# A fused attention and two-layer mixture kernel: ranks by counting matmuls, a short token chunk in two products, a tile's pieces in another order

## The chip, the core and the metric

The kernel runs on one core of one Trainium2 chip. The metric is the device time of one execution in microseconds; lower is better. TensorE (PE) multiplies, VectorE (DVE), ScalarE (ACT) and GpSimd (POOL) work element by element, SyncE (SP) starts most transfers. Each engine takes its instructions strictly in program order and waits at each for the semaphores of what it needs.

## What is computed

Three layers follow one another: thresholded attention, a mixture of eight experts with a sticky routing, and a mixture of four causal attention experts. The second is the one that the change touches:

```python
for b in range(4):                       # x: 4 x 576 tokens of 512
    prev_e = -1
    for s in range(576):
        fresh_e = int(np.argmax(logits[b, s]))
        if s == 0 or local_gate[b, s] < 0.5:
            e = fresh_e
        else:
            e = prev_e if prev_e >= 0 else fresh_e
        prev_e = e
        h = np.maximum(x[b, s] @ w1[e], 0.0)     # 512 -> 1024
        out[b, s] = p[e] * (h @ w2[e])           # 1024 -> 512
```

So a token either takes the expert of its own largest logit or keeps the one of the token before it, and only the chosen expert's two layers are computed for it.

## The kernel before

**Stage 1** runs attention on 16 pairs of heads. An order written out by hand gives every step of a pair a due time in units of one score tile, nine to a pair; due times sort the instructions of all engines. For one pair the scores go to one of three score banks (line 246), VectorE takes the row's extreme (257) and, when ScalarE has the exponentials (267), forms the kept values (280), which frees the bank. TensorE transposes them (293) into a pool of two banks that everything else of stage 1 shares, ScalarE evicts them (304), and TensorE multiplies by the values (336). A product with the identity and the gate weights (368) turns the result into token rows and logits; ScalarE evicts it (386), and GpSimd scales it by the reciprocal sums (393), which line 357 on GpSimd and line 360 on VectorE prepare. The last pair does that scaling of the logits on VectorE (384).

**The early routing** (`Route.early`) handles the first three batches while stage 1 still computes the fourth. It is a list of steps, each with a due time in `EARLY`; a step that yields a second part (an eviction) has two. A pair of 24-row tables (three batches by eight experts, 576 tokens long) is scanned into a one-hot table O of each token's expert (line 609). The running count of O along the tokens is a second scan, in two halves (617). Three small matmuls (624 to 626) give the totals; `most` (639 to 650) finds the most frequent expert, whose number `e0` starts the loads of the first tile's weights (`W0`, line 952), and six values `n0` that limit the tiles. `value` and `place` (655 to 672) pick each token's rank by five matmuls; `split_rank` splits it into a row and a column of a tile; `column` and `hot` (680 to 698) make one-hot tables on GpSimd; `invert` (704, 705) multiplies them into token numbers, by which GpSimd gathers the first tile's rows.

**The last routing** (`Route.main`) adds the fourth batch. The chain on VectorE is long, and TensorE fills it with pieces of the first expert tile: 16 pieces of the first layer, 16 of the second, each a handful of products. `FILL` says how many go between two steps. The remaining ones are dealt out by `LEFT`: before each of the three transposes (`tx`, line 984) of the second tile's gathered chunks, pieces run until so many are left. The second of these transposes takes a bank of a PSUM pool that opens where the router's own pool closes; the last read of the router's pool is line 873 on VectorE.

**The expert tiles** hold 256 tokens, or 288 (the first of the second kind) and 352. Every product is done in three passes of a split number: high by high, high by low, low by high. `g1` computes the first layer, `hT_ev` evicts it as high and low halves (ScalarE 1006, VectorE 1007), `y_mm` (1040) computes the second layer with a chunk of at most 128 tokens as the stationary side and 512 columns streamed, `y_ev` evicts and stores it.

## Time and profile before

| | us |
|---|---|
| three runs | 756.20, 756.21, 756.98 |
| median | 756.21 |
| the profiled execution, its own time | 758.47 |
| its span | 756.7 |
| TensorE busy in the span | 727.2 (96%) |
| VectorE, ScalarE, GpSimd busy | 545.3, 490.3, 285.6 |

The span is what the trace covers of one execution; the rest of its time lies around it. A busy TensorE is a modelled figure: products overlap, so the distance from one start to the next is the cost of one, not its duration. In the timelines a row gives start, busy time, engine, line, operation, what it writes and reads, shapes and count, and in square brackets the idle time ahead of it with what released it.

### The profile page before, as it was taken

The page shows a single profiled execution, that of the slowest core. Times are in us where ns is not written, and L with a number is a line of the kernel's source. Part 1 is how long each engine was busy: PE and PEld are TensorE (multiplying, and loading weights), DVE is VectorE, ACT ScalarE, POOL GpSimd, SP SyncE. Part 2 cuts the span into 40 slices and gives each one's busy share as a digit, 9 for nine tenths or more (in the row PEclk, how much of TensorE's full clock was granted, in tenths as well). Part 3 has the DMA queues.
Part 4 walks back from the last instruction along what each step waited for, and adds up shares of the span by engine and source line. Part 5 has one row for each costly group of instructions (what it writes and reads, how often), then busy time and mean ns, then how long its engine had stood idle before and what let it go on. Part 6 is the DMA issues. An engine that isn't in the chain of part 4 may idle for free.

```text
span 756.7 us, 14216 instructions
## 1 busy us (share of the span) xinstructions
PE 727.2 (96%) x5061; PEld 614.3 (81%) x5061; DVE 545.3 (72%) x1424; ACT 490.3 (65%) x1024; POOL 285.6 (38%) x435
## 2 busy tenths in 40 slices
PE   5999999999999898899999999999999999999996
PEld 4787888888887677697899899889888888888874
DVE  6998998999988987713745555654268888887781
ACT  5888887888887685223555455544256877777783
POOL 6888888888776880300101000100156000000000
PEclk9999999999999999999999999999999999999998
DMA  8439443443432620295457647701233000100103
GB/s 278 145 116 316 139 141 122 159 131 114 130 114 65 239 62 17 84 367 176 160 201 248 219 168 261 261 0 53 61 105 102 10 16 1 43 15 29 43 29 102
DMA packets 37408, 95.40 MB, mean 126 GB/s; under 512 B 4336, under 2 KB 14832, under 8 KB 33232
## 3 DMA queue, kind: packets, MB, share of 16 engines
q1 hardware_dynamic: 30960, 73.62, 28.3%
q0 software_dynamic: 5360, 19.34, 8.2%
q10 hardware_dynamic: 1008, 1.44, 0.6%
q8 instruction: 42, 0.69, 0.4%
q14 instruction: 38, 0.31, 0.1%
HBM read 75.58 MB, written 18.81 MB: 125 GB/s over the span
## 4 chain that ended last, share of the span: by engine, by line
PE 85%; DVE 7%; ACT 3%; issue 2%; DMA 1%; ACTq 0%; DVEq 0%; POOLq 0%
PE py L1040 16%; PE acc L1015 15%; PE Y L336 10%; PE S L246 8%; PE X L293 8%; PE AV L1599 4%; PE X L1548 3%; PE Y L368 2%; PE S L251 2%; PE misc L1361 1%; PE S L1479 1%; PE S L1478 1%; PE misc L1363 1%; PE misc L1362 1%; DVE P L280 1%
## 5 line engine op out<-in xcount | busy, mean ns | idle before, releaser
L280 DVE SCALAR_TENSOR_TENSOR P<-S,nm,E 128x576 f32<-128x576 f32 x144 | 116.1, 814 | 10.2 <-ACT E L267 4.3
L257 DVE TENSOR_REDUCE nm<-S 128x1 f32<-128x576 f32 x144 | 105.8, 752 | 17.1 <-PE S L246 16.2
L267 ACT ACTIVATE E<-S,nm 128x576 f32<-128x576 f32 x144 | 104.0, 746 | 10.8 <-DVE nm L257 10.1
L246 PE MATMUL S<-KK,QS 128*128 128x288 f32 x256 | 84.0, 343 | 9.6 <-ACT KK L192 5.9
L293 PE MATMUL X<-cst,P 128*128 128x128 f32 x576 | 87.1, 278 | 1.6 <-ACT PT L304 0.7
L1730 POOL DMA_INDIRECT xg<-x_dram,inv x22 | 23.6, 1071 | 168.9 <-PE px L984 147.6
L293 PEld LDWEIGHTS X<-cst,P 128*128 128x128 f32 x576 | 67.0, 141 | 16.9 <-issue 7.4
L304 ACT ACTIVATE PT<-X 128x512 f32<-128x512 f32 x128 | 75.5, 604 | 3.7 <-PE X L293 1.0
L1015 PE MATMUL acc<-xTh,w1l 128*128 128x256 f32 (+2 forms) x256 | 76.7, 300 | 0.0
L1015 PE MATMUL acc<-xTh,w1h 128*128 128x256 f32 (+2 forms) x256 | 76.6, 299 | 0.0
L1015 PE MATMUL acc<-xTl,w1h 128*128 128x256 f32 (+2 forms) x256 | 76.4, 298 | 0.0
L246 PE MATMUL S<-KL,QS 128*128 128x288 f32 x256 | 73.3, 300 | 0.3 <-DVE KL L201 0.3
L1040 PE MATMUL py<-w2h,hTh 128*128 128x512 f32 (+2 forms) x176 | 71.8, 408 | 0.0
L1007 DVE SCALAR_TENSOR_TENSOR hTl<-acc,hTh 128x352 fp32r<-128x352 f32 (+2 forms) x52 | 29.8, 575 | 57.1 <-ACT hTh L1006 57.1
L336 PE MATMUL Y<-PT,v 128*64 128x320 f32 (+1 forms) x512 | 69.1, 412 | 1.6 <-ACT PM L325 0.8
L1040 PE MATMUL py<-w2l,hTh 128*128 128x512 f32 (+2 forms) x176 | 70.0, 398 | 0.0
L1040 PE MATMUL py<-w2h,hTl 128*128 128x512 f32 (+2 forms) x176 | 69.7, 396 | 0.0
L1006 ACT ACTIVATE hTh<-acc 128x352 fp32r<-128x352 f32 (+2 forms) x52 | 26.2, 506 | 56.9 <-PE acc L1015 56.9
L246 PEld LDWEIGHTS S<-KK,QS 128*128 128x128 f32 x256 | 49.6, 194 | 11.5 <-ACT KK L192 5.9
L336 PEld LDWEIGHTS Y<-PT,v 128*64 128x64 f32 x512 | 33.8, 136 | 26.2 <-issue 4.8
L246 PEld LDWEIGHTS S<-KL,QS 128*128 128x128 f32 x256 | 49.9, 195 | 0.6 <-DVE KL L201 0.6
L1799 POOL DMA_INDIRECT raw<-yg,slot x18 | 17.5, 975 | 85.7 <-DMA yg<-y 62.4
(383 smaller groups left out, 1986.7 us busy)
## 6 DMA issues: line engine op xcount, KB each, us to landing
raw<-in_w_dram SPq DMA_DIRECT2D x32, 1024.0 KB, 6.7
kraw<-in_kT_dram SPq DMA_DIRECT2D x15, 608.0 KB, 4.1
QS<-in_qT_dram POOLq DMA_DIRECT2D x15, 576.0 KB, 5.9
v<-in_vp_dram SPq DMA_DIRECT2D x16, 320.0 KB, 3.0
yg<-y SPq DMA_DIRECT2D x17, 256.0 KB, 5.7
qraw<-in_qx_dram SPq DMA_DIRECT2D x15, 288.0 KB, 2.9
x_dram<-xr SPq DMA_DIRECT2D x16, 256.0 KB, 2.4
yg<-raw SPq DMA_DIRECT2D x1, 3072.0 KB, 13.0
```

The costliest lines, as they stand in the source:

```text
L246: nc.tensor.matmul(o, QS[p % NQ][:, a, cs], k[i][:, sl(576 * a)], start=(n == 0), stop=(n == 1))
L257: nc.vector.tensor_reduce(nm[:, 0:1], t[:, :, :288], axis=AX.XY, op=ALU.min)
L267: nc.scalar.activation(e, t[:, :, :288], AF.Exp, scale=-1.0, bias=nm[:, 0:1])
L280: nc.vector.scalar_tensor_tensor(PP[p, c][:, S * a:S * a + S].rearrange("p (h n) -> p h n", h=2), t[:, :, :288], nm[:, 1:2], e, op0=ALU.is ...
L293: nc.tensor.transpose(x[:, 128 * kc:128 * kc + 128], pp[:, o:o + 128], ident)
L304: nc.scalar.activation(PT[p, h][:, a, :, f:f + 128], x.rearrange("p (k q) -> p k q", k=4), AF.Copy)
L336: nc.tensor.matmul(out, l, r, start=s, stop=e, skip_group_check=True)
L1006: nc.scalar.activation(hh, p, AF.Relu)
L1007: nc.vector.scalar_tensor_tensor(hl, p, 0.0, hh.bitcast(F32), op0=ALU.max, op1=ALU.subtract)
L1015: nc.tensor.matmul(o, a[:, fs], x[:, k, 0:w], start=(first and n == 0), stop=(k == 3 and n == 2), skip_group_check=True)
L1040: nc.tensor.matmul(ys[t][u][0:m], h, w[:, 512 * f:512 * f + 512], start=(i == 0 and f == 0 and n == 0), stop=(i == 3 and f == 1 and n == 2))
L1599: nc.tensor.matmul(o[half(a), f:NH[h]], l, r, start=(k == 0), stop=(k == (1, 4)[h]), skip_group_check=True)
```

## The change

Three things. The running count of O is no longer scanned: O is copied to bf16 (with its sums along the way), turned by five matmuls so that tokens lie along the partitions, and counted by matmuls with a triangle and with ones; VectorE reads the product with one multiplication and one sum. The rank is split by rounding on GpSimd; the choice of the most frequent expert is cut in two, its six limits moved to a later due time. The second layer of the 288-wide tile's last chunk, 32 tokens, puts the high and the low half side by side as 64 stationary columns, so that two products stand for three; the halves are added at eviction. And `LEFT` deals out the first tile's pieces differently.

```diff
-        v = self.nc.vector
+    def split_rank(self, r, i, bs, v):
...
-        def ranks(i):
-            def f(*_):
...
-                v.tensor_tensor_scan(R[rs, c], K["ones"][rs, 0:1].to_broadcast([N, HS]), O[rs, c], R[rs, HS - 1:HS] if i else 0.0,
-                                     op0=ALU.mult, op1=ALU.add)
-            return f
...
+        def flat(*_):
+            aux = T["aux"] = E.tile([128, 376], BF16, name="aux", tag="w1h", bufs=4)
+            gp.tensor_scalar(aux[:, 0:128], K["maskS"], 0.0, 1.0, op0=ALU.is_lt, op1=ALU.mult)
+            gp.memset(aux[:, 128:256], 1.0)
+            sl = T["sl"] = E.tile([128, 2, 5, B], F32, name="sle")
+            gp.memset(sl, -1.0)
+
+        def counted(*_):
+            O = T["O"]
+            OB = T["OB"] = self.scratch("OB", BF16, 640)
+            n = T["n"] = E.tile([32, 1], F32, name="ne")
+            gp.memset(OB[rs, S:640], 0.0)
+            nc.scalar.activation(OB[rs, :S], O[rs], AF.Copy, accum_out=n[rs])
+
+        def turn(xt, _):
+            t = xt()
+            for j in range(5):
+                mm(t[:, N * j:N * j + N], T["OB"][rs, 128 * j:128 * j + 128], K.identb[rs, 0:N], start=(j == 0), stop=(j == 4),
+                   skip_group_check=True)
+            return lambda: nc.scalar.activation(T["aux"][:, 256:376], t[:, 0:120], AF.Copy)
...
         def count(xt, _):
-            n = T["R"][rs, S - 1:S]
...
+            n, aux = T["n"][rs], T["aux"]
+            ot = aux[:, 256:376].rearrange("p (j r) -> p j r", j=5)
             sm = xt()
...
-            mm(sm[0:32, 0:1], K["m2"][rs], n, start=True, stop=True, skip_group_check=True)
-            mm(sm[0:32, 1:2], K["m1"][rs], n, start=False, stop=True, skip_group_check=True)
-            mm(sm[0:32, 8:16], n.to_broadcast([N, 32]), K["selE"][rs], start=False, stop=True, skip_group_check=True)
...
+            mm(sm[:, 0:120], aux[:, 0:128], aux[:, 256:376], start=True, stop=False, skip_group_check=True)
+            for j in range(4):
+                mm(sm[:, N * j + N:120].rearrange("p (j r) -> p j r", r=N), aux[:, 128:256],
+                   ot[:, j].unsqueeze(1).to_broadcast([128, 4 - j, N]), start=False, stop=False, skip_group_check=True)
+            mm(sm[:, 0:120].rearrange("p (j r) -> p j r", r=N), n.to_broadcast([N, 128]),
+               K["m2"][rs, 0:N].unsqueeze(1).to_broadcast([N, 5, N]), start=False, stop=True, skip_group_check=True)
+            mm(sm[0:32, 129:130], K["m1"][rs], n, start=False, stop=True, skip_group_check=True)
+            mm(sm[0:32, 136:144], n.to_broadcast([N, 32]), K["selE"][rs], start=False, stop=True, skip_group_check=True)
+            t = T["t"] = X.tile([32, 32], F32, name="te")
+            T["sm"] = sm
...
             def out():
...
-                v.tensor_copy(t[:, 0:1], sm[0:32, 0:1])
-                v.tensor_scalar(t[:, 16:17], sm[0:32, 1:2], 16.0, K["prefrow"][0:32], op0=ALU.mult, op1=ALU.add)
-                v.scalar_tensor_tensor(t[:, 8:16], sm[0:32, 8:16], 16.0, K["prefer"][0:32], op0=ALU.mult, op1=ALU.add)
...
+                sf = T["sf"] = E.tile([32, 4], BF16, name="sf")
+                v.tensor_scalar(t[:, 16:17], sm[0:32, 129:130], 16.0, K["prefrow"][0:32], op0=ALU.mult, op1=ALU.add)
+                v.scalar_tensor_tensor(t[:, 8:16], sm[0:32, 136:144], 16.0, K["prefer"][0:32], op0=ALU.mult, op1=ALU.add)
+                v.tensor_reduce(t[:, 1:2], t[:, 8:16], axis=AX.X, op=ALU.max)
+                v.tensor_scalar(t[:, 2:3], t[:, 16:17], t[:, 1:2], None, op0=ALU.is_equal)
+                v.tensor_scalar(sf[rs], K["selb"][rs], t[rs, 2:3], None, op0=ALU.mult)
             return out
...
+        def ranks(*_):
+            sl, aux, sm = T["sl"], T["aux"], T["sm"]
+            pr = E.tile([128, 120], F32, name="pr", tag="w1h", bufs=4)
+            v.tensor_tensor(pr, sm[:, 0:120], aux[:, 256:376], op=ALU.mult)
+            v.tensor_reduce(sl[:, 0, :, 0:3], pr.rearrange("p (j b e) -> p j b e", j=5, b=3), axis=AX.X, op=ALU.add)
+            q, one = self.rq, 1.5 * 2.0 ** 23
+            gp.tensor_scalar(q, sl[:, 0], -63.5, 1.0 / 128.0, op0=ALU.add, op1=ALU.mult)
+            gp.tensor_scalar(q, q, one, 1.0, op0=ALU.add, op1=ALU.mult)
+            gp.tensor_scalar(q, q, -one, 1.0, op0=ALU.add, op1=ALU.mult)
+            gp.tensor_scalar(self.place, q, -128.0, 1.0, op0=ALU.mult, op1=ALU.mult)
+            gp.tensor_tensor(self.place, self.place, sl[:, 0], op=ALU.add)
+
         def most(*_):
-            t, ti = T["t"], E.tile([32, 2], I32, name="mi")
-
-            v.tensor_reduce(t[:, 1:2], t[:, 8:16], axis=AX.X, op=ALU.max)
-            v.tensor_scalar(t[:, 2:3], t[:, 16:17], t[:, 1:2], None, op0=ALU.is_equal)
+            t, ti = T["t"], X.tile([32, 2], I32, name="mi")
+            T["mi"] = ti
             v.tensor_copy(ti[:, 0:1], t[:, 1:2])
             v.tensor_scalar(ti[:, 1:2], ti[:, 0:1], 4, None, op0=ALU.arith_shift_right)
             v.tensor_scalar(ti[:, 0:1], ti[:, 0:1], 15, None, op0=ALU.bitwise_and)
             v.tensor_scalar(self.e0, ti[:, 0:1], -1.0, 8.0, op0=ALU.mult, op1=ALU.add)
+
+        def taken(*_):
+            t, ti = T["t"], T["mi"]
...
-        def value(*_):
...
-            v.tensor_scalar(V[rs, S:640], K["ones"][rs, 0:1].to_broadcast([N, 64]), 0.0, None, op0=ALU.mult)
-            gp.tensor_scalar(V[rs, :S], T["R"][rs], t[rs, 0:1], 1.0, op0=ALU.add, op1=ALU.mult)
-            gp.tensor_tensor(V[rs, :S], V[rs, :S].bitcast(F32), T["O"][rs], op=ALU.mult)
...
         def place(xt, _):
             ps = xt()
             for j in range(5):
-                mm(ps[:, 8 * j:8 * j + 8], T["V"][rs, 128 * j:128 * j + 128], T["sf"][rs],
-                   start=(j == 0), stop=(j == 4), skip_group_check=True)
...
+                mm(ps[:, 4 * j:4 * j + 4], T["OB"][rs, 128 * j:128 * j + 128], T["sf"][rs], start=(j == 0), stop=(j == 4),
+                   skip_group_check=True)
...
             def out():
-                v.tensor_scalar(sl, ps[:, 0:40].rearrange("p (j g b) -> p g j b", j=5, g=2), -1.0, None, op0=ALU.add)
-                self.split_rank(sl[:, 0], i, slice(0, 4))
+                o = T["sl"][:, 1, :, 0:3]
+                v.scalar_tensor_tensor(o, T["sl"][:, 0, :, 0:3], 1.0, ps[:, 0:20].rearrange("p (j b) -> p j b", j=5)[:, :, 0:3],
+                                       op0=ALU.add, op1=ALU.mult)
+                v.tensor_scalar(o, o, -1.0, None, op0=ALU.add)
...
-        return [copies, *self.choose_steps(slice(0, 3), gp), rows("A", 1), rows("G", 0), rest, scan(0), scan(1), ranks(0), ranks(1),
-                count, most, value, place, column, *[hot(k) for k in range(5)], invert]
+        return [copies, *self.choose_steps(slice(0, 3), gp), rows("A", 1), rows("G", 0), rest, flat, scan(0), scan(1), counted, turn,
+                count, ranks, most, taken, place, column, *[hot(k) for k in range(5)], invert]
...
+    def packed(t):
+        c = chunks(t)[-1]
+        return c.stop - c.start if c.stop - c.start <= 64 else 0
+
+    def low(t, c):
+        w, m = width(t), packed(t)
+        o = w if m and c.stop == w else w + m + c.start
+        return slice(o, o + c.stop - c.start)
...
-            hT[t].append(tuple(W.tile([128, 2, NL], F32R, name="hT" + q, bufs=4) for q in "hl"))
-        w = width(t)
-        hh, hl = (q[:, n:, 0:w] if w == 256 else q[:, n, 0:w] for q in hT[t][i])
+            hT[t].append(W.tile([128, 2, 2 * NL], F32R, name="hT", bufs=4))
+        w, m = width(t), packed(t)
+        h = hT[t][i][:, n:] if w == 256 else hT[t][i][:, n]
         p = p[:, 0:512].rearrange("p (f t) -> p f t", f=2) if w == 256 else p[:, 0:w]
-        nc.scalar.activation(hh, p, AF.Relu)
-        nc.vector.scalar_tensor_tensor(hl, p, 0.0, hh.bitcast(F32), op0=ALU.max, op1=ALU.subtract)
+        nc.scalar.activation(h[..., 0:w], p, AF.Relu)
+        for c in (slice(0, w - m), slice(w - m, w)):
+            if c.stop > c.start:
+                nc.vector.scalar_tensor_tensor(h[..., low(t, c)], p[..., c], 0.0, h[..., c].bitcast(F32), op0=ALU.max, op1=ALU.subtract)
...
     def y_mm(t, i, u, f):
         wh, wl = wc[t, 4 + i]
-        hh, hl = (q[:, f, chunks(t)[u]] for q in hT[t][i])
-        m = hh.shape[-1]
-        for n, (h, w) in enumerate(((hh, wh), (hh, wl), (hl, wh))):
-            nc.tensor.matmul(ys[t][u][0:m], h, w[:, 512 * f:512 * f + 512], start=(i == 0 and f == 0 and n == 0),
-                             stop=(i == 3 and f == 1 and n == 2))
+        c = chunks(t)[u]
+        l = low(t, c)
+        ops = [(c, wh), (c, wl), (l, wh)]
+        if l.start == c.stop and packed(t):
+            ops = [(slice(c.start, l.stop), wh), (c, wl)]
+        for n, (k, w) in enumerate(ops):
+            m = k.stop - k.start
+            nc.tensor.matmul(ys[t][u][0:m], hT[t][i][:, f, k], w[:, 512 * f:512 * f + 512], start=(i == 0 and f == 0 and n == 0),
+                             stop=(i == 3 and f == 1 and n == len(ops) - 1), skip_group_check=True)
...
-        nc.scalar.activation(y[0:m], ys[t][u][0:m], AF.Copy)
+        if s.stop == width(t) and packed(t):
+            lo = W.tile([128, DM], F32, name="ylo", tag="xg", bufs=4)
+            nc.scalar.activation(lo[0:m], ys[t][u][m:2 * m], AF.Copy)
+            nc.vector.tensor_tensor(y[0:m], ys[t][u][0:m], lo[0:m], op=ALU.add)
+        else:
+            nc.scalar.activation(y[0:m], ys[t][u][0:m], AF.Copy)
...
-EARLY = (60, 123.4, 123.42, 123.44, 123.46, 124.2, 124.25, (124.55, 125), (125.65, 126.1), (126.12, 126.4), 126.7, 127.2, 127.8, 127.82,
-         (129.25, 129.55), 129.7, 129.9, (131.58, 131.95), 132, 133, 134.5, 136, 137.5, 139, (141.1, 141.4))
-W0 = 129.8
+EARLY = (60, 123.4, 123.42, 123.44, 123.46, 124.2, 124.25, (124.55, 125), (125.65, 126.1), (126.12, 126.4), 126.5, 126.7, 127.2, 127.8,
+         (129.25, 129.45), (129.5, 130.6), 130.65, 130.93, 146.5, (132, 132.36), 132.38, 133, 134.5, 136, 137.5, 139, (141.1, 141.4))
+W0 = 130.95
...
-LEFT = (13, 12, 9)
+LEFT = (13, 9, 4)
```

TensorE at the end of the early part of stage 1, where the counts are formed: `R` is the running count, `OB` the bf16 copy of O, `aux` holds the triangle, the ones and the turned table, `ne` the totals.

```order
-L626 MATMUL Y<-cst,R 32x8
-L293 MATMUL X<-cst,P 128x128 x4
+L628 LDWEIGHTS OB
+L628 MATMUL Y<-identb,OB 128x24
...
+L293 MATMUL X<-cst,P 128x128 x4
+L636 LDWEIGHTS aux
+L636 MATMUL Y<-aux 128x120
...
+L640 MATMUL Y<-cst,ne 128x120
+L642 MATMUL Y<-ne,cst 32x1
+L643 MATMUL Y<-cst,ne 32x8
 L336 MATMUL Y<-PT_3462,v 64x320 x8
```

Three matmuls became five ahead of the transposes and eight between them and the products of line 336.

VectorE at the end of stage 1, before the change: `rc` are the reciprocal sums, `lg` the last pair's logits.

```order
L280 SCALAR_TENSOR_TENSOR P,sM<-S,nm,E 128x576
L899 TENSOR_TENSOR w1l<-raw_72,w1h 128x1024
L360 RECIPROCAL rc<-rc 128x10
L384 TENSOR_TENSOR lg<-Y,rc 128x36
L896 CAST w2h<-raw_74 128x1024
```

The same place in the changed kernel: `n` are the six limits.

```order
L921 TENSOR_TENSOR w1l<-raw_72,w1h 128x1024
L360 RECIPROCAL rc<-rc 128x10
L678 TENSOR_SCALAR n_86<-mi,te 32x1
L679 TENSOR_SCALAR n_86<-te 32x1
L680 TENSOR_TENSOR n_86<-n_86 32x1
L681 COPY n_86<-te 32x1
L682 TENSOR_SCALAR n_86<-te 32x1
L683 TENSOR_SCALAR n_86<-te 32x1
L384 TENSOR_TENSOR lg<-Y,rc 128x36
```

The six operations stood right behind the choice of the expert; now they stand between the reciprocal and the logits.

TensorE as the last routing ends, before the change: `px` and `py` written from `xg` are the transposes of the first and second gathered chunk, the others products of the first tile's second layer.

```order
L984 MATMUL px_4576<-cst_62,xg_4477 128x128 x4
L1040 MATMUL py_4505<-w2h_4194,hTh_4346 128x512
L1040 MATMUL py_4505<-w2l_4195,hTh_4346 128x512
L1040 MATMUL py_4505<-w2h_4194,hTl_4347 128x512
L984 MATMUL py_4590<-cst_62,xg_4479 128x128 x4
```

The same place in the changed kernel.

```order
L1006 MATMUL px_4586<-cst_62,xg_4489 128x128 x4
...
L1077 MATMUL py_4516<-w2h_4537,hT_4416 128x512
L1077 MATMUL py_4516<-w2l_4538,hT_4416 128x512
L1077 MATMUL py_4516<-w2h_4537,hT_4416 128x512 x2
L1077 MATMUL py_4516<-w2l_4538,hT_4416 128x512
L1077 MATMUL py_4516<-w2h_4537,hT_4416 128x512
L1077 MATMUL py_4517<-w2h_4537,hT_4416 128x512
L1077 MATMUL py_4517<-w2l_4538,hT_4416 128x512
L1077 MATMUL py_4517<-w2h_4537,hT_4416 128x512
L1006 MATMUL py_4609<-cst_62,xg_4491 128x128 x4
```

One piece of three products stood between the two; now there are four (the first, like the one before the change, is left out here). Between the second and the third transposes there were three pieces and are five, behind the third nine and four.

## Rows read from the trace of the kernel before

**Rows 1.** Busy time by stretch (us from the span's start), all engines, clock, DMA.

```profile
235.00:262.00 27.00, 23.09 (x173) 17.57 (x172) 24.97 (x72) 16.80 (x33) 20.42 (x34) 1.00 0.38 146
...
311.80:326.30 14.50, 12.32 (x52) 9.59 (x51) 5.63 (x19) 2.07 (x4) 4.09 (x5) 0.88 0.55 167
...
316.10:318.80 2.70, 2.70 (x9) 2.13 (x8) 1.34 (x2) 0.60 (x1) 0.94 (x1) 0.51 0.28 88
```

**Rows 2.** Timeline of TensorE, early routing: start, busy, idle before and releaser.

```profile
247.27 0.40 PE L246 MATMUL S<-KK,QS 128*128 128x288 f32 x1 [1.59 <-DVE P L280]
...
248.00 0.22 PE L624 MATMUL Y<-R,cst 24*32 24x1 f32 x2
...
249.62 2.37 PE L336 MATMUL Y<-PT,v 128*64 128x320 f32 x16 [0.69 <-ACT PT L304]
...
253.67 0.69 PE L665 MATMUL Y<-sf,Ve 24*128 24x8 f32 x5
...
256.59 0.66 PE L293 MATMUL X<-cst,P 128*128 128x128 f32 x4 [0.27 <-DVE sle L672]
...
259.08 0.53 PE L251 MATMUL S<-KK,QM 128*128 128x288 f32 x2 [0.62 <-DVE P L280]
```

**Rows 3.** Timelines of VectorE, then of GpSimd, in the early routing.

```profile
243.75 0.90 DVE L617 TENSOR_TENSOR_SCAN R<-cst,O 24x288 f32<-24x288 f32 x1
...
244.69 1.80 DVE L617 TENSOR_TENSOR_SCAN R<-cst,R,O 24x288 f32<-24x288 f32 x1
...
250.90 1.00 DVE L647 TENSOR_TENSOR n<-n 32x1 f32<-32x1 f32 x1
...
244.14 1.75 POOL L204 TENSOR_TENSOR KL<-kraw,KK 128x576 fp32r<-128x576 f32 x1
...
250.47 1.41 POOL L660 TENSOR_TENSOR Ve<-Ve,O 24x576 fp32r<-24x576 f32 x1
```

**Rows 4.** Timelines of TensorE, then of ScalarE, in the last routing.

```profile
303.00 0.28 PE L801 MATMUL po<-SB,OB 32*128 32x44 bf16 x5
...
296.93 0.68 ACT L753 ACTIVATE OB<-O 32x576 bf16<-32x576 f32 x1 [0.82 <-DVE O L752]
```

**Rows 5.** Timelines of GpSimd, then of VectorE, to the end of stage 1.

```profile
256.63 0.80 POOL L680 TENSOR_SCALAR fe<-sle 128x20 f32<-128x20 f32 x3 [1.35 <-DVE sle L672]
...
275.23 1.11 POOL L1730 DMA_INDIRECT xg<-x_dram,inv  x1 [0.87 <-DVE inv L705]
...
283.69 0.20 POOL L357 TENSOR_SCALAR rc<-RS 128x10 f32<-128x10 f32 x1
...
283.93 0.22 DVE L360 RECIPROCAL rc<-rc 128x10 f32<-128x10 f32 x1 [0.83 <-POOL rc L357]
284.78 0.19 DVE L384 TENSOR_TENSOR lg<-Y,rc 128x36 f32<-128x36 f32 x1 [0.63 <-PE Y L368]
```

**Rows 6.** Timelines of SyncE's queue, then of ScalarE: first tile's weights.

```profile
251.73 2.12 SPq L952 DMA_DIRECT2D raw<-in_w_dram  x4
...
269.23 1.05 ACT L898 ACTIVATE w1h<-raw 128x1024 fp32r<-128x1024 f32 x1
```

**Rows 7.** Timelines of TensorE, then of VectorE, as routing ends.

```profile
312.18 0.48 PE L1040 MATMUL py<-w2h,hTh 128*128 128x512 f32 x1
...
315.32 1.09 PE L984 MATMUL py<-cst,xg 128*128 128x128 f32 x4 [2.18 <-issue]
...
319.55 0.43 PE L984 MATMUL px<-cst,xg 32*128 32x32 f32 x4
319.91 0.50 PE L1040 MATMUL py<-w2h,hTh 128*128 128x512 f32 x1
...
326.31 0.30 PE L1015 MATMUL acc<-xTh,w1h 128*128 128x288 f32 x1
...
314.96 0.26 DVE L873 TENSOR_TENSOR ex<-po,ex 128x160 f32<-128x160 f32 x1
```

**Rows 8.** Line 1040, 339 to 356 us: min/median/max ns, starts, forms.

```profile
L1040 PE MATMUL py<-w2l,hTh x23: 387/395/399, 339.3 to 355.5; 128*128 128x512 f32 x16, 128*32 128x512 f32 x7
```

More of the change, by code (lines that the diff above doesn't have):

```diff
@@ L664, in place @@
             for j in range(5):
-                mm(ps[:, 8 * j:8 * j + 8], T["V"][rs, 128 * j:128 * j + 128], T["sf"][rs],
-                   start=(j == 0), stop=(j == 4), skip_group_check=True)
-            sl = T["sl"] = E.tile([128, 2, 5, B], F32, name="sle")
-            i = E.tile([128, 2, 5, B], I32, name="ie")
+                mm(ps[:, 4 * j:4 * j + 4], T["OB"][rs, 128 * j:128 * j + 128], T["sf"][rs], start=(j == 0), stop=(j == 4),
+                   skip_group_check=True)
             def out():
-                v.tensor_scalar(sl, ps[:, 0:40].rearrange("p (j g b) -> p g j b", j=5, g=2), -1.0, None, op0=ALU.add)
-                self.split_rank(sl[:, 0], i, slice(0, 4))
+                o = T["sl"][:, 1, :, 0:3]
+                v.scalar_tensor_tensor(o, T["sl"][:, 0, :, 0:3], 1.0, ps[:, 0:20].rearrange("p (j b) -> p j b", j=5)[:, :, 0:3],
+                                       op0=ALU.add, op1=ALU.mult)
+                v.tensor_scalar(o, o, -1.0, None, op0=ALU.add)
             return out
@@ L797, in main @@
         v.tensor_scalar(rk, ps[:, :, 1:2], -1.0, None, op0=ALU.add)
-        self.split_rank(rk, W.tile([128, 2, 5, 1], I32, name="ik"), slice(3, 4))
+        self.split_rank(rk, W.tile([128, 2, 5, 1], I32, name="ik"), slice(3, 4), v)
         pp = PS.tile([128, 512], F32, name="po", tag="pa")[:, 0:220].rearrange("p (j x) -> p j x", j=5)
```

10 lines of the change are left out of this document (removed).

## Prediction

> **What bounds the kernel now.** I read the busy times by stretch first. TensorE is busy nearly everywhere, so only two things shorten the run: columns that it need not stream, and stretches in which it stands still or runs at its lower clock. The stretch 235 to 262 us, where the early routing runs inside the end of the attention stage, has 23.09 us of work in 27.00: 3.91 us idle. The stretch 311.8 to 326.3, where routing ends and the first expert tile finishes, has 12.32 in 14.50, and from 316.1 to 318.8 the granted clock is 0.51, so the lower of its two levels (1.2 instead of 2.4 GHz) [rows 1].
>
> Then the timeline of TensorE, row by row, for who released each wait. Four waits belong to the early routing: 1.59 us before the scores at 247.27 (for the keep of line 280, which frees a score bank), 0.69 at 249.62, 0.27 at 256.59 and 0.62 at 259.08 [rows 2], together 3.17 of the 3.91. VectorE's timeline says why the longest stands there: the two rank scans of line 617 take 0.90 and 1.80 us and stand ahead of that keep [rows 3]. The second hole is one wait of 2.18 us at 315.32, ahead of the transposes of the second gathered chunk [rows 7]. Its releaser is given only as "issue", so I took it from times: those transposes write a bank of the pool that opens when the router's PSUM pool closes, and the last reader of that pool is line 873 on VectorE, 314.96 + 0.26 = 315.22, a tenth ahead of the start. The six products that follow run at the lower clock.
>
> **The change, part by part.**
>
> *Early routing.* Out of VectorE's queue go both rank scans (2.70 us), the long split of ranks, the fill and half of the small chain; the six operations for the tile limits move behind line 360. With 2.70 us less ahead of it the keep that frees the bank ends before TensorE asks for it, so the 1.59 goes. Between the transposes and the attention-times-v products, where TensorE waited 0.69 for ScalarE to evict, now stand the counting matmuls: that wait is covered. The 0.27 waited for a VectorE result that is now a short read of the placing matmuls, and the 0.62 for a keep that stands behind some 5 us less. I take all four as gone: 3.17.
>
> TensorE's work: out go lines 624 to 626 (0.22 for the first pair, three pairs partly on top of each other, about 0.3) and line 665 (0.69) [rows 2], so 0.99. In come two groups of five small bf16 products, of the form of line 801 (0.28 for five [rows 4]), 0.56; five with 24 to 120 columns, at most twice that by the larger stationary side, taken at 0.4; and three fp32 ones, about 0.3 like the three that go. Net 0.27 more.
>
> New waits: TensorE now waits in order for four things, the turned counts from ScalarE, the read of the counting bank by VectorE (it blocks the next but one tile in the two-bank pool), the selection, and the read of the placing bank. ScalarE's added eviction is a 24x576 copy, nearest row 0.68 us [rows 4], beside 10.2 us of idle time in the stretch (27.00 less 16.80 [rows 1]). VectorE's new product and sum over 120 columns are nearest to line 873's 0.26 each [rows 7]. The chain of seven small operations is about 1.5 us and TensorE has about 3 us of products (line 336's 2.37 us [rows 2] and its neighbours) between the count and the tile that needs the bank. So 0 if VectorE is at the keep ahead of it in time, and 1.6 (a wait as long as the longest removed) if it is late by all of it. I take 0.3, nearer the low end, since the scans that made VectorE late are gone.
>
> GpSimd takes the split: five operations on 128x20, nearest 0.20 each [rows 5], and three fills; it loses two passes over 24x576, of which line 660 alone is 1.41 [rows 3]. Its work there is balanced, and 1.35 us of waiting for `sle` [rows 5] mostly go. Its place in line is what counts: GpSimd works without a gap from 256.63 on, and the last row of that run, line 357 at 283.69, releases line 360 on VectorE, behind which the six moved operations now stand ahead of line 384, which feeds ScalarE's eviction and TensorE's next tile. Line 360 is done by 284.15 before the change, and line 384 then waits 0.63 us more, for TensorE [rows 5]. GpSimd gets ahead by about 1.7 (the earlier `sle`) plus the 0.87 that it waited for `inv` [rows 5], so 2.6; the six operations cost between 0.6 and 6 x 0.22 = 1.3, of which 0.63 fit into the idle time. TensorE is ahead by about 2.6 as well. So between 0 and 0.7 is lost here; I take 0.3. Early routing: 3.17 - 0.27 - 0.3 - 0.3 = **2.3 us**, bounds 0.6 (3.17 - 0.27 - 1.6 - 0.7) and 3.2 (no new wait, no work added on balance).
>
> The weight loads of the first tile start after the expert is known, about 1.5 us later than at 251.73; their first reader on ScalarE is at 269.23 [rows 6], and by then four loads of 1 MB have long landed. The load of v on SyncE moves ahead of them and waits for nothing of the router any more. Cost 0.
>
> *First tile's pieces dealt out.* The order above shows one piece (three products) between the first and the second transposes before, and four after. A piece at the full clock is 27 products in 326.31 - 319.91 = 6.40 us [rows 7], so 0.237 each, 0.71 a piece. From 312.18 to 326.31 TensorE now spends 14.13 us on 13 pieces and two sets of transposes. The work alone is 13 x 0.71 + 2 x 0.36 (as the third set: 319.91 less 319.55) = 9.9. Four pieces end at 312.18 + 2.84 = 315.0, line 873 lets go at 315.22, so about 0.3 of the hole stays: 10.2. The gain is **3.9 us**: 2.1 of waiting filled, and the rest is the lower clock not met, since what is left of the hole is far shorter than the 1.59 us at 247.27, behind which the clock stayed up (1.00 in that stretch [rows 1]). Bounds: 4.1 if nothing of the hole stays, 2.2 if the clock falls all the same. The pieces that are moved up read what VectorE splits ahead of line 873 in its own order; the transposes of the third chunk move from 319.55 to about 319.2, and its eviction has four pieces (2.8 us) ahead of its first reader.
>
> *Last 32 tokens in two passes.* Only the 288-wide tile has a last chunk that fits twice. For it each of 4 x 2 steps drops one of three products: the two halves of the hidden values stand side by side as 64 stationary columns. The products with 32 stationary columns cost what those with 128 do, 0.395 us each at the median [rows 8], so they stream their 512 columns at 0.237 each like the rest: 8 x 0.237 = **1.9 us**. Bounds 1.5 and 1.9. The price is on engines with room: a second subtraction for each of eight evictions on VectorE, and at the end a copy and an addition of 32x512. The wait for the output buffer's store passes from ScalarE to VectorE, where the next subtraction and one split of weights stand behind it; both have four accumulators and a whole first layer of slack ahead of their readers. Cost 0.
>
> Sum: 2.3 + 3.9 + 1.9 = 8.1. The profiled execution took 758.47, of which 756.7 is its span; that becomes 750.4. It lies 2.26 above the median of the runs, 756.21, and since all three terms are differences I take them from the median: **748.1 us**.
>
> **A rule weighed.** GpSimd's two-input pass of line 660 ran from 250.47 to 251.88, and VectorE's two-input operation of line 647 on 32x1, which its neighbours do in under 0.2, took 1.00 and ended with it; the second rank scan ended with line 204's pass in the same way (244.14 + 1.75 = 245.89, and the scan that began at 244.69 took 1.80 where its twin took 0.90) [rows 3]. The Trainium skill, SBUF — State Buffer, section "Who interferes with whom", says that the port pair which VectorE shares with GpSimd is an exclusive lock, so that one of the two blocks fully. The trace agrees with it in these rows. The rule speaks against the change, which moves work onto GpSimd's side of that lock: by it the early routing would give 0.7 instead of 2.3 (the first rival).
>
> **The rivals.** First, VectorE's new chain is held up by GpSimd's passes as line 647 was: the selection or the sum over 120 columns stretches by 1.0, the bank of the counts is read late and the tile behind it, then the placing, wait in turn: 2.3 - 1.6 = 0.7 remains of the early routing, 749.7. For it: GpSimd's pass of line 209 stands just there. Against: the new operations read PSUM or one SBUF operand, and of such ones none was stretched. This is the lock of the Trainium skill's page above, and the chance is what the rows show of it here. Second, the clock: something else than the length of the hole took it down, and the three pieces run at 1.2 GHz although the hole is filled: 3.9 - 1.7 gives 749.8. Third, the change does not do what it says: the packed product's 64 columns or the second accumulation cost as much as what they replace, 1.9 less: 750.0. Fourth, on the other side: the four hand-offs to an in-order TensorE each open a wait. It decides against the change when they are 2.2 us on average (a hole of that length also cost 1.7 us of clock at 315.32): 4 x 2.2 + 1.7 = 10.5 against 8.1 plus nothing: 758.6. For it: VectorE is at 24.97 of 27.00 in that stretch before the change [rows 1]. Against: about 5 us leave it there.
>
> **How the numbers follow.** Forecast, 747.0 to 749.4: 0.62. VectorE held up, 749.7: 0.17. The clock, 749.8: 0.08. Two passes without gain, 750.0: 0.05. Slower, 758.6: 0.03. Better than 747.0: 0.05. The range goes to the first three rivals and to the sum's bound of 9.2 on the other side: 746.8 to 750.4. A measurement of this kernel tells 0.2% (1.5 us) from no change; all but the fourth rival and a small part of mixed cases are faster by more: faster 0.94, same 0.03, slower 0.03.
>
> **What would show it.** Right: no wait above 0.5 us on TensorE between 245 and 256; the transposes of the second chunk start within 0.4 of the piece ahead of them and the clock reads 1.00 from there; TensorE has 8 products less; line 384's counterpart starts two to three microseconds earlier. Wrong: a wait for VectorE ahead of the transposes behind the counting or the placing products; the clock at 0.5 after 312; a wait at the tile behind line 384's counterpart that grows by more than 0.7.

## The result, and the profile after

The changed kernel took 749.89 us in the median of five runs (748.61 to 751.0), the kernel before 756.98 in the same comparison (756.2 to 760.51): ratio 0.9897, 95% interval 0.987 to 0.9924, so 7.8 us less (5.8 to 9.8). 748.1 was forecast, in a range of 746.8 to 750.4. The total came out as predicted. Two of its three terms did not.

The profiled execution of the changed kernel took 751.0, of which 749.2 is its span. Busy time by stretch, with the granted clock of TensorE three columns from the end (the three rows answer [rows 1], but the last is another stretch, since the low clock now stands elsewhere):

```profile
235.00:262.00 27.00, 26.04 (x212) 20.03 (x212) 23.93 (x67) 20.68 (x43) 21.51 (x43) 1.00 0.39 144
...
311.80:326.30 14.50, 14.41 (x85) 12.31 (x84) 4.91 (x20) 3.31 (x7) 2.65 (x3) 1.00 0.65 212
...
283.20:287.20 4.00, 3.96 (x18) 1.92 (x20) 3.05 (x3) 2.36 (x3) 0.00 (x0) 0.57 0.00 0
```

The two stretches with holes are full: TensorE idles 0.96 us of the first instead of 3.91, and 0.09 of the second instead of 2.18. This execution also has a stretch at about half clock that was not there, from 283.2 to 287.2.

TensorE's timeline in the early routing and to the end of stage 1 (answers [rows 2]):

```profile
244.47 0.29 PE L246 MATMUL S<-KL,QS 128*128 128x288 f32 x1
244.86 0.44 PE L317 MATMUL Y<-cst,P 128*128 128x128 f32 x2
245.13 0.33 PE L320 MATMUL Y<-iq 128*128 128x64 f32 x2
245.28 0.38 PE L246 MATMUL S<-KK,QS 128*128 128x288 f32 x1
...
245.98 0.28 PE L628 MATMUL Y<-identb,OB 24*128 24x24 bf16 x5
...
246.92 0.21 PE L636 MATMUL Y<-aux 128*128 128x120 bf16 x1
...
247.80 2.37 PE L336 MATMUL Y<-PT,v 128*64 128x320 f32 x16
...
251.66 0.66 PE L368 MATMUL Y<-iq,XT 128*128 128x146 f32 x4
...
252.78 0.27 PE L688 MATMUL Y<-sf,OB 24*128 24x4 bf16 x5
...
254.80 0.60 PE L293 MATMUL X<-cst,P 128*128 128x128 f32 x4
255.15 0.51 PE L251 MATMUL S<-KK,QM 128*128 128x288 f32 x2
...
275.54 0.66 PE L293 MATMUL X<-cst,P 128*128 128x128 f32 x4 [0.25 <-ACT xraw L386]
...
281.82 0.66 PE L1791 MATMUL Y<-cst,xg 128*128 128x128 f32 x4 [0.65 <-ACT xraw L386]
283.24 4.04 PE L336 MATMUL Y<-PT,v 128*64 128x320 f32 x16 [0.76 <-ACT PM L325]
```

No row between 245 and 256 names a wait; the four of [rows 2] are gone. The row with 0.25 at 275.54 stands at 279.50 in the trace of before. The last row shows what the half clock costs in this execution: sixteen products of line 336 that take 2.37 us at 247.80 take 4.04 at 283.24.

VectorE's timeline, the new short operations and the end of stage 1 (answers the VectorE rows of [rows 5]):

```profile
249.76 0.26 DVE L659 TENSOR_TENSOR pr<-Y,aux 128x120 f32<-128x120 f32 x1
250.06 0.28 DVE L660 TENSOR_REDUCE sle<-pr 128x15 f32<-128x120 f32 x1
...
277.91 1.34 DVE L921 TENSOR_TENSOR w1l<-raw,w1h 128x1024 fp32r<-128x1024 f32 x1 [0.61 <-ACT w1h L920]
280.44 0.22 DVE L360 RECIPROCAL rc<-rc 128x10 f32<-128x10 f32 x1 [1.19 <-POOL rc L357]
280.57 0.14 DVE L678 TENSOR_SCALAR n<-mi,te 32x1 f32<-32x1 int32 x1
...
281.06 0.17 DVE L384 TENSOR_TENSOR lg<-Y,rc 128x36 f32<-128x36 f32 x1
```

The product and the sum that take the scans' place need 0.26 and 0.28 us, not stretched. Line 384 no longer waits for TensorE; the six operations from 280.57 on stand ahead of it.

TensorE as the last routing ends (answers [rows 7]):

```profile
309.77 0.60 PE L1006 MATMUL px<-cst,xg 128*128 128x128 f32 x4
...
312.78 0.40 PE L1077 MATMUL py<-w2h,hT 128*128 128x512 f32 x1
313.26 0.63 PE L1006 MATMUL py<-cst,xg 128*128 128x128 f32 x4
...
320.56 0.30 PE L1048 MATMUL acc<-xTh,w1h 128*128 128x288 f32 x1
```

From 312.78 a product takes 0.23, so what is left of the hole ahead of 313.26 is 0.25 us; 0.3 was expected. The short chunk's products by form, 315 to 360 us (answers [rows 8]):

```profile
L1077 PE MATMUL py<-w2l,hT 128*32 128x512 f32 x8 | 3.2, 395 | 0.0
L1077 PE MATMUL py<-w2h,hT 128*64 128x512 f32 x8 | 3.1, 389 | 0.0
```

Sixteen instead of twenty-four, and the ones with 64 stationary columns cost what the others do.

### The profile page after: what moved, and what is told of

Read it like the earlier page. It is cut to its first block, busy times and chain, and to the rows that moved or that the text cites. A ratio compares the mean times of both kernels' runs of the same rounds, so it can differ in the third digit from the quotient of the medians.

```text
span 749.2 us, 14233 instructions
## 1 busy us (share of the span) xinstructions
PE 724.0 (97%) x5063; PEld 611.9 (82%) x5063; DVE 544.6 (73%) x1426; ACT 490.7 (66%) x1027; POOL 283.6 (38%) x442
## 4 chain that ended last, share of the span: by engine, by line
PE 85%; DVE 6%; ACT 4%; DMA 1%; issue 1%; POOL 1%; ACTq 0%; POOLq 0%; DVEq 0%
PE py L1077 16%; PE acc L1048 15%; PE Y L336 11%; PE S L246 9%; PE X L293 8%; PE AV L1641 4%; PE X L1590 3%; PE Y L368 2%; PE S L251 2%; PE S L1520 1%; PE S L1521 1%; PE misc L1672 1%; PE px L1006 1%; PE misc L1671 1%; PE misc L1673 1%
## 5 line engine op out<-in xcount | busy, mean ns | idle before, releaser
L280 DVE SCALAR_TENSOR_TENSOR P<-S,nm,E 128x576 f32<-128x576 f32 x144 | 116.3, 815 | 10.2 <-ACT E L267 4.5
L1077 PE MATMUL py<-w2h,hT 128*128 128x512 f32 (+2 forms) x344 | 114.8, 400 | 0.0
L1077 PEld LDWEIGHTS py<-w2h,hT 128*128 128x128 f32 (+2 forms) x344 | 63.0, 183 | 15.4
L336 PE MATMUL Y<-PT,v 128*64 128x320 f32 (+1 forms) x512 | 70.8, 420 | 0.9 <-ACT PM L325 0.8
L1077 PE MATMUL py<-w2l,hT 128*128 128x512 f32 (+2 forms) x176 | 69.4, 394 | 0.0
L1037 ACT ACTIVATE hT<-acc 128x352 fp32r<-128x352 f32 (+2 forms) x52 | 26.2, 507 | 56.9 <-PE acc L1048 53.1
L1040 DVE SCALAR_TENSOR_TENSOR hT<-acc,hT 128x352 fp32r<-128x352 f32 (+3 forms) x60 | 30.4, 519 | 44.5 <-ACT hT L1037 44.5
```

What stands on the lines that cost most here:

```text
L280: nc.vector.scalar_tensor_tensor(PP[p, c][:, S * a:S * a + S].rearrange("p (h n) -> p h n", h=2), t[:, :, :288], nm[:, 1:2], e, op0=ALU.is ...
L336: nc.tensor.matmul(out, l, r, start=s, stop=e, skip_group_check=True)
L1037: nc.scalar.activation(h[..., 0:w], p, AF.Relu)
L1040: nc.vector.scalar_tensor_tensor(h[..., low(t, c)], p[..., c], 0.0, h[..., c].bitcast(F32), op0=ALU.max, op1=ALU.subtract)
L1077: nc.tensor.matmul(ys[t][u][0:m], hT[t][i][:, f, k], w[:, 512 * f:512 * f + 512], start=(i == 0 and f == 0 and n == 0), stop=(i == 3 and f ...
```

## The experiments: one table

All kernels run the same stages, so the distance between the starts of the same TensorE instructions can be set side by side. The marks are: the first products of line 317 behind 196 us; the row of line 293 with the wait for `xraw` (275.54 above); the first product of the first expert tile; the first transposes of the second tile (309.77); the second tile's first product (320.56); the third tile's first product; the end of the span. "Fall" is the place where the granted clock goes to its lower level, 1.2 GHz, and stays there for some products (the end of the run, where TensorE has no more products, is left out).

| kernel | start to 203 | early routing | end of stage 1 | last routing | deal | second tile | rest | fall |
|---|---|---|---|---|---|---|---|---|
| before | 203.11 | 76.39 | 11.67 | 20.66 | 14.48 | 30.37 | 400.02 | 315 |
| e8, before again | 201.96 | 76.35 | 11.68 | 20.70 | 14.38 | 30.38 | 401.05 | 314 |
| e9, before again | 201.63 | 76.37 | 11.67 | 20.67 | 12.92 | 30.37 | 400.87 | 248 |
| e11, before again | 202.00 | 76.39 | 11.67 | 22.08 | 11.52 | 30.38 | 401.26 | 307 |
| e4, before, new deal | 202.22 | 76.33 | 11.67 | 20.69 | 10.80 | 30.36 | 401.23 | 249 |
| changed | 202.64 | 72.90 | 13.57 | 20.66 | 10.79 | 28.44 | 400.20 | 283 |
| e7, changed again | 202.90 | 72.98 | 11.87 | 20.67 | 10.80 | 28.45 | 398.93 | none |
| e10, changed again | 202.44 | 72.92 | 11.77 | 20.67 | 10.80 | 28.45 | 399.35 | none |
| e12, changed again | 202.80 | 72.91 | 11.79 | 20.65 | 10.80 | 28.44 | 399.01 | none |
| e1, limits behind line 384 | 202.62 | 72.93 | 11.68 | 22.09 | 10.51 | 28.45 | 399.52 | 304 |
| e2, changed, old deal | 201.72 | 72.88 | 11.80 | 20.69 | 12.90 | 28.44 | 399.87 | 15 |
| e3, changed, three passes | 202.27 | 72.92 | 11.79 | 20.65 | 10.81 | 30.35 | 398.61 | none |
| e5, routing alone | 202.90 | 72.91 | 11.77 | 22.05 | 11.51 | 30.35 | 400.01 | 305 |
| e6, copies later | 202.29 | 72.99 | 11.46 | 20.95 | 10.80 | 28.45 | 398.76 | none |

Each of the five stages between the first column and "rest" repeats within some 0.1 us between kernels that share it, except where a fall stands in it. So the parts of the change are read off directly, and so is each fall. The first column and the last do not repeat like that: they spread by 1.5 and 1.2 us within the kernel before alone.

## What the clock's fall belongs to

After the first comparison the theory was that the six operations ahead of line 384, which lengthen the wait at 281.82 from 0.43 to 0.65 us, let the clock fall at 283. The rival was chance.

**e1** moves them behind line 384:

```diff
-         (129.25, 129.45), (129.5, 130.6), 130.65, 130.93, 146.5, (132, 132.36), 132.38, 133, 134.5, 136, 137.5, 139, (141.1, 141.4))
+         (129.25, 129.45), (129.5, 130.6), 130.65, 130.93, 146.75, (132, 132.36), 132.38, 133, 134.5, 136, 137.5, 139, (141.1, 141.4))
```

> The changed kernel with one due time altered: the six operations on the tile limits (lines 678 to 683) stand behind line 384 on VectorE instead of ahead of it; nothing else moves on any engine. Theory: they lengthen TensorE's wait ahead of the first tile's transposes (line 1791) from 0.43 to 0.65 us, and that is what lets the granted clock fall behind the next wait, at 283.24, where sixteen products of line 336 took 4.04 us instead of 2.37. Then the wait is 0.43 again, the sixteen products take 2.4 and the clock reads 1.00 from 283 to 287; about 1.9 us less than the changed kernel (span about 747.3, some 9.4 under the span of before). Rival: the fall has nothing to do with the six operations (stage 1 now reaches this point 4 us earlier, or it comes by chance): the wait is 0.43, the sixteen products still take 4.0, and only 0.2 us are gained.

Measured: 749.05 us, ratio to before 0.9889 (0.9875 to 0.9903). TensorE's timeline:

```profile
281.61 0.66 PE L1791 MATMUL Y<-cst,xg 128*128 128x128 f32 x4 [0.43 <-ACT xraw L386]
283.03 2.37 PE L336 MATMUL Y<-PT,v 128*64 128x320 f32 x16 [0.76 <-ACT PM L325]
...
304.46 0.20 PE L759 MATMUL prest<-q,cst 32*1 32x23 f32 x2 [0.23 <-DVE q L858]
304.51 0.18 PE L759 MATMUL prest<-tf,cst 32*1 32x2 f32 x2
304.63 0.54 PE L1048 MATMUL acc<-xTPh,w1h 128*128 128x256 f32 x1
```

The wait is 0.43 and the sixteen products take 2.37, as the theory has it; but a fall now stands at 304, behind a wait of 0.23 us, where 256-column products take 0.41 to 0.42 each from the next row on instead of 0.28. The theory explains the wait, not the fall.

**e7, e10, e12** are the changed kernel unaltered, for three more profiles.

> The changed kernel, unaltered, for a second profile. If the clock's fall at 283 is fixed by the program (the wait of 0.65 us ahead of it), it stands at the same place, and the stage there takes 13.6 us. If each execution has about one fall of 1.7 us at one of several short waits, it stands elsewhere or nowhere, and the stage takes 11.8.

> The changed kernel, unaltered, for a third profile. By the same theory: with no fall 748.3 (as the second profile), with a fall of 1.7 us at 283 or 305 about 750 to 751 (as the first, 751.0).

> The changed kernel, unaltered, for a fourth profile: as for the third.

They took 748.34, 748.15 and 748.22 us. TensorE's timeline of e7:

```profile
282.13 0.66 PE L1791 MATMUL Y<-cst,xg 128*128 128x128 f32 x4 [0.62 <-ACT xraw L386]
283.55 2.38 PE L336 MATMUL Y<-PT,v 128*64 128x320 f32 x16 [0.76 <-ACT PM L325]
```

Nearly the same waits, 0.62 and 0.76, and no fall; there is none in e10 and e12 either. So the program does not fix the one at 283: it came in one profile of four. It cost 13.57 less 11.8, or 1.8 us. That execution took 751.0 against 748.15 to 748.34; the other microsecond of the difference lies in the last column.

**e8, e9, e11** are the kernel before unaltered.

> The kernel before, unaltered, for a second profile. If the fall behind the wait of 2.18 us belongs to that wait, the six products behind it are at the lower clock again and the distance from the first transposes of line 984 to the second tile is 14.5 us; if it came by chance, 12.9, and the fall stands elsewhere or nowhere.

> The kernel before, unaltered, for a third profile. Both profiles so far have the fall behind the 2.18 us wait and lie 1.1 to 2.3 us above the median of the timed runs (758.47, 758.34 against 756.2 to 757.2). If the median execution has no fall that costs time, a profile without it takes some 756.6 to 757; with one at 315 some 758.4. If the fall there is part of every execution, it stands here too and the time is at the median.

> The kernel before, unaltered, for a fourth profile: as for the third.

They took 758.34, 756.36 and 757.14 us. TensorE's timeline of e8, where the wait of 2.19 is followed by the lower clock (1.08 us for four transposes):

```profile
314.19 1.08 PE L984 MATMUL py<-cst,xg 128*128 128x128 f32 x4 [2.19 <-issue]
```

and of e9, where the fall stands at 248 (4.06 us for the sixteen products that take 2.37) and the wait of 2.18 is followed by the full clock (0.63):

```profile
248.16 4.06 PE L336 MATMUL Y<-PT,v 128*64 128x320 f32 x16 [0.69 <-ACT PT L304]
...
313.83 0.63 PE L984 MATMUL py<-cst,xg 128*128 128x128 f32 x4 [2.18 <-DVE ex L873]
```

and of e11, where the fall stands at 307 and the wait is only 0.80:

```profile
314.24 0.63 PE L984 MATMUL py<-cst,xg 128*128 128x128 f32 x4 [0.80 <-issue]
```

Two things follow. A wait of 2.2 us stood ahead of the second chunk's transposes in three of the four profiles of the kernel before; two of them show the lower clock behind it, one does not. And a fall costs time only where TensorE is what everything waits for. At 248 it costs nothing: the early routing takes 76.37 with it and 76.39 without, since VectorE set the pace there. At 307 it costs nothing either: last routing and deal take 22.08 + 11.52 = 33.60 with it and 20.67 + 12.92 = 33.59 without, the hole shrinking by what the products lose. In e1, where the new deal has filled the hole, a fall at the same place costs 22.09 + 10.51 less 20.67 + 10.80, or 1.1 us. At 315 it costs 14.38 - 12.92 = 1.5. The two executions with that loss took 758.47 and 758.34, the two without 756.36 and 757.14.

## The parts of the change

**e4**, the kernel before with the new deal alone:

```diff
-LEFT = (13, 12, 9)
+LEFT = (13, 9, 4)
```

> The kernel before with LEFT = (13, 9, 4) and nothing else. By the sum: 3.7 to 3.9 us faster than before; the wait ahead of the second chunk's transposes is 0.2 to 0.4 us, the clock reads 1.00 from 311 to 327. Rival: the deal pays only together with the early routing (pieces not ready because their weights or halves come later in the kernel before), under 2.5. Its stage 1 is that of before, with a wait of 0.43 ahead of the first tile's transposes: the clock is expected at 1.00 there.

Measured: 755.35 us (12 runs), ratio 0.9973 (0.9961 to 0.9986), so 2.0 us less (1.1 to 3.0). That is the rival's number, though not for its reason: the deal works alone as well as with the rest, 10.80 us in both.

**e2**, the changed kernel with the old deal, the same line the other way round.

> The changed kernel with LEFT = (13, 12, 9) as before. If the deal of pieces is worth what the two traces show (14.48 us against 10.79 from the first transposes of line 1006 to the second tile), this is 3.7 us slower than the changed kernel, with one wait of about 2 us ahead of the second chunk's transposes and the six products behind it at the lower clock. Rival: with the last routing's chain unchanged and TensorE 2 us earlier the hole is filled or cheaper, under 2.5 us. Stage 1 is that of the changed kernel: if the clock's fall at 283 belongs to it, it stands here too; if it came by chance, it need not.

Measured: 750.61 us, ratio 0.9911 (0.9899 to 0.9924). TensorE's timeline:

```profile
307.09 0.60 PE L1006 MATMUL px<-cst,xg 128*128 128x128 f32 x4
...
310.59 0.63 PE L1006 MATMUL py<-cst,xg 128*128 128x128 f32 x4 [2.20 <-issue]
...
319.99 0.30 PE L1048 MATMUL acc<-xTh,w1h 128*128 128x288 f32 x1
```

The hole of 2.20 is there, the lower clock behind it is not (this execution had its fall at 15 us). The stage takes 12.90 against 10.80: without a fall the deal is worth 2.1 us. The expectation of 3.7 failed by the clock.

**e3**, the changed kernel with three products for the 32 tokens:

```diff
     def packed(t):
         c = chunks(t)[-1]
-        return c.stop - c.start if c.stop - c.start <= 64 else 0
+        return 0
```

> The changed kernel with the last chunk of 32 tokens in three products again (no 64-column stationary side, no added halves). The distance from the second tile's first product to the third tile's grows by 8 x 0.237 = 1.9 us, and the time by the same. Rival: the packed form had hidden costs on VectorE and ScalarE behind the tile (second subtraction, copy and addition), then the loss is under 1.2. The clock at 283 is read as in the run ahead.

Measured: 750.40 us, ratio 0.9916 (0.9903 to 0.9929). The second tile takes 30.35 instead of 28.44, so 1.9 us, as expected.

**e5**, e2 and e3 together, so that the early routing alone is left.

> The changed kernel with the deal LEFT = (13, 12, 9) and the three products for the 32 tokens as before, so that the early routing alone is left of the change. By TensorE's landmarks of the runs so far (76.36 us before and 72.90 after from the diagonal transposes at 203 to the wait of 0.25 at 275, less 0.12 for the six operations) it is 3.3 us faster than before: ratio 0.9956. By the prediction's own term it is 2.3 (0.9970). Rival: part of the 3.3 is taken back later, since the stage behind it does not start earlier for being reached earlier; under 1.5 us then. The distances of the stages are expected at 72.9, 11.8, 20.7, 12.9 and 30.4 us where the clock does not fall, and 1.4 to 1.9 more in the one where it does.

Measured: 753.39 us, ratio 0.9952 (0.9937 to 0.9967), so 3.6 us less (2.5 to 4.8). This time alone cannot decide between 3.3 and the prediction's 2.3, since e5 also holds the 1.1 us of changed code that the sum did not have (below): 4.4 and 3.4 were to be compared with it, and both lie in the interval. The stages decide it. They came as expected, the last routing with a fall at 305 that the hole behind it gave back (22.05 + 11.51 = 33.56).

**e6** puts e1's due time and that of the four scaled copies of line 411 later, since ScalarE's 1.07 us there looked like the cause of the 0.76 us wait:

```diff
-        at(g + 11.95, norm_last)
+        at(g + 12.3, norm_last)
...
-         (129.25, 129.45), (129.5, 130.6), 130.65, 130.93, 146.5, (132, 132.36), 132.38, 133, 134.5, 136, 137.5, 139, (141.1, 141.4))
+         (129.25, 129.45), (129.5, 130.6), 130.65, 130.93, 146.75, (132, 132.36), 132.38, 133, 134.5, 136, 137.5, 139, (141.1, 141.4))
```

> The changed kernel with two due times altered at the end of stage 1: the six limit operations behind line 384 on VectorE, and the four scaled copies of line 411 on ScalarE behind the evictions of line 325 and of the first tile's transposes (line 1796) instead of ahead of them. Theory: ScalarE's 1.07 us at line 411 is what TensorE waits for in the 0.76 us ahead of the last sixteen products of line 336; that wait falls below 0.1, the distance from the 0.25 wait at 275 to the first product of the first tile goes from 11.8 to about 10.9, and the kernel is 0.8 to 0.9 us faster than the changed one (ratio to before about 0.988 or less). Rival: line 411's rows are stored and read back by the routing soon after, so that a wait for the store (0.28 us at 296.4 in the changed kernel) grows by as much as is gained.

Measured: 747.60 us, ratio 0.988 (0.9862 to 0.9898). The time is the lowest of all, but the reordering is not why. TensorE's timeline, then ScalarE's:

```profile
281.92 2.37 PE L336 MATMUL Y<-PT,v 128*64 128x320 f32 x16
...
285.98 1.01 PE L368 MATMUL Y<-iq,XT 128*128 128x146 f32 x6 [0.56 <-ACT XT L348]
...
287.72 0.39 PE L1048 MATMUL acc<-xTPl,w1h 128*128 128x256 f32 x1 [0.61 <-DVE xTPl L1797]
```

```profile
282.65 1.06 ACT L411 ACTIVATE xr<-xraw,rc 128x64 f32<-128x64 f32 x4
283.62 1.04 ACT L920 ACTIVATE w1h<-raw 128x1024 fp32r<-128x1024 f32 x1
284.57 1.04 ACT L920 ACTIVATE w2h<-raw 128x1024 fp32r<-128x1024 f32 x1
285.52 0.41 ACT L348 ACTIVATE XT<-Y 128x320 f32<-128x320 f32 x1
```

The wait of 0.76 is gone. The copies now push two weight conversions later, and the eviction of line 348 has to stand behind them, so TensorE waits 0.56 at 285.98 and 0.61 instead of 0.33 at 287.72. End of stage 1 and last routing together take 11.46 + 20.95 = 32.41, against 11.79 + 20.65 = 32.44 in e12 and 11.68 + 20.66 = 32.34 that e1 shows without its fall (its own first stage, and the last routing of the others). Neither theory nor rival: the wait moved along ScalarE's queue, not to the store. Its ratio lies inside the interval of e1's and of the changed kernel's, so no better version is claimed.

## Why the prediction came out

**Early routing: mechanism right, 2.3 forecast, 3.3 measured.** 76.37 less 72.91 is 3.46, less 0.12 at the end of stage 1 (11.79 against 11.67). All four waits are gone from the rows. The three charges set against them came out as follows.

- *Net work of 0.27*: from start to start the turn takes 0.22, the counts 0.88, the placing 0.20, together 1.30; out went 0.28 and 0.62. So 0.40 more; but the four products of line 368, which took 0.79 behind line 665 (254.29 to 255.08 in the trace of before), take 0.40 (251.66 to the next at 252.06). Net nothing.
- *0.3 for a new hand-off*: no row names one, since idle times of about 0.1 us get no bracket, but the starts show one. Line 317 now comes 0.39 behind the last product of line 246 (244.47 to 244.86), for 0.13 before, so 0.26 more. It waits for line 304's eviction on ScalarE, which now has the copy of O (line 623, 0.67 us) ahead of it. The charge was about right.
- *0.3 at line 384*: 0.12, since GpSimd got further ahead than the 2.6 that was put down (line 357 starts at 280.20 for 283.69, of which 0.47 is the earlier start of the whole stage).

The waits themselves were worth more than their brackets, which count from the modelled end of the product ahead. TensorE in the trace of before:

```profile
245.00 0.29 PE L246 MATMUL S<-KL,QS 128*128 128x288 f32 x1
245.13 0.38 PE L317 MATMUL Y<-cst,P 128*128 128x128 f32 x2
245.35 0.33 PE L320 MATMUL Y<-iq 128*128 128x64 f32 x2
...
257.81 0.66 PE L293 MATMUL X<-cst,P 128*128 128x128 f32 x4
```

From line 320 to the scores behind the 1.59 took 1.92 us (245.35 to 247.27) and takes 0.15 now: 1.77 given back. From the transposes to line 251 behind the 0.62 took 1.27 (257.81 to 259.08) and takes 0.35 (254.80 to 255.15): 0.92. So 3.17 is too small by at least 0.48, and 3.17 + 0.48 - 0.26 - 0.12 = 3.27, close to the 3.3 measured. That 3.3 is just above the upper bound of 3.2. The term was mis-sized in two steps: the waits were taken at their brackets, and work was charged that came out at nothing.

**First tile's pieces: 3.9 forecast, 2.1 measured without a fall, 3.6 with one.** The filling of the hole went as worked out (0.25 left of it for 0.3; 10.43 us from 310.13 to 320.56 for 10.2). The step that failed is "the rest is the lower clock not met", with the comparison to the 1.59 us wait behind which the clock stayed up: the clock's fall was taken for a property of the wait, and a bound of 2.2 "if the clock falls all the same" was set for the wrong case. The fall is not tied to this wait; in e9 it stands elsewhere and costs nothing. With it fails a sentence of the sum: "since all three terms are differences I take them from the median". The profiled execution lay 2.26 above the median, and 1.5 of that was this very fall. A loss that the profiled execution had was deducted from a median that lies at the executions without it (756.36 and 757.14); which of the timed runs had such a fall is not known.

**Last 32 tokens: 1.9 forecast, 1.92 measured** (30.37 less 28.44). No wait at the buffer's store or behind VectorE's added operations shows.

**What the sum did not hold.** Behind the third tile's first product the changed kernels are 1.1 us faster: from there to the first product of the last tile they take 160.3 us instead of 161.1, and that tile's first layer saves another 0.3. The first layer of the fourth tile, for one, takes 11.30 us instead of 11.51. By form, in that stretch of before:

```profile
L1015 PE MATMUL acc<-xTh,w1l 128*128 128x256 f32 x32 | 9.1, 285 | 0.0
L1015 PE MATMUL acc<-xTl,w1h 128*128 128x256 f32 x32 | 9.1, 283 | 0.0
```

and of the changed kernel:

```profile
L1048 PE MATMUL acc<-xTh,w1l 128*128 128x256 f32 x32 | 9.0, 280 | 0.0
L1048 PE MATMUL acc<-xTl,w1h 128*128 128x256 f32 x32 | 8.9, 279 | 0.0
```

Same products, same count, a few nanoseconds each. The gain is in every kernel with the changed code, e3 and e5 too, and not in e4. So it needs neither the two passes nor the deal; whether the routing or the new tile that holds both halves of the hidden values brings it (by where the operands then lie) was not tried and stays open.

So the terms are 3.3, 2.1, 1.9 and 1.1: 8.4 us without a fall on either side, where 8.1 was forecast and 7.8 (5.8 to 9.8) measured. The total was right because a term too small by 1.0 and a gain that was not seen, 1.1, made up for one too large by 1.8. What follows the tiles differs by about a microsecond between executions of one kernel (the last column is 400.02 to 401.26 for the kernel before); where that comes from was not followed.

**The rivals.** VectorE held up by GpSimd did not happen: lines 659 and 660 ran at their normal length. The lock is there all the same. GpSimd's timeline of the changed kernel, beside VectorE's line 921 above (277.91 to 279.25):

```profile
278.24 1.14 POOL L423 TENSOR_TENSOR lg<-lg 128x45 f32<-128x45 f32 x1
279.46 0.28 POOL L424 TENSOR_TENSOR L<-L,lg 128x45 f32<-128x45 f32 x1
```

An operation on 45 elements takes 1.14 us until VectorE's two-input pass is over, and its twin 0.28. It lies ahead of line 357, and its 0.86 us more than the twin's are most of the 1.19 that VectorE waits at line 360. The Trainium skill, SBUF — State Buffer, section "Who interferes with whom", says that a VectorE instruction with two inputs in SBUF contends with a GpSimd instruction that reads SBUF, and that issue order decides which of the two blocks. The rows agree, in the direction that the prediction did not weigh: here GpSimd is the one that waits. The change did not bring this: in the kernel before it was line 424 that took 1.31 us, from 281.93 on, beside VectorE's line 899 (281.87 to 283.10). The second rival, the clock, came true in another place than it named: where a fall costs something, as at 283, the changed kernel takes 751.0. The third falls with the rows by form above: a product with 64 stationary columns takes 389 ns. The slower case, hand-offs of 2.2 us each, showed in no row.

## What to carry to other kernels

Before a loss in a profile is booked as a gain, see whether the profiled execution stands above the median by about that loss: if so it may be an accident of that execution, and a second profile of the unchanged kernel decides it for the price of one run. Set the same instructions of several traces side by side as distances; stages that repeat to a tenth of a microsecond show parts of 0.1 us where run times with a spread of one or two do not. When a wait is removed from an in-order engine, look at what its queue now puts late: e6 removed 0.76 us and got nearly all of it back two instructions later.

## What the runs showed of the hardware that was not expected

The granted clock falls at one place or at none in each of these executions: once in nine of the fourteen profiles, not at all in five, and in each of the nine the missing clock, summed over stretches of 1 us, is 1.70 or 1.71 us. Every fall stands at or behind a wait, but the length of the wait does not decide: 0.23 us in e1 was followed by one, 2.20 in e2 and 2.18 in e9 were not, and in those two executions a fall had come earlier. Two profiles of the same kernel put it at 315 and 248. The Trainium skill, TensorE: Matmul & The Clock Gate, section "HAM oscillation — how this bites in real kernels", lays a lower clock in mid-kernel to idle gaps between groups of products, in its example waits for transfers that are longer than any wait here. That each fall here stands at or behind an idle gap agrees; that gaps of 0.2 to 2.2 us bring one in some executions and not in others goes beyond it. What chooses the gap no run here shows.
